# Banded attention before a bilinear feed-forward: from steps of two head pairs by 256 queries to steps of all heads by 128 queries, and from TensorE transposes of the probabilities to 32x32 block transposes on VectorE

## The chip, the cores and the metric

The kernel runs on one core of one Trainium2 chip. The metric is the device time of one execution in microseconds (us). TensorE (PE) multiplies matrices and loads their stationary operand (PEld), VectorE (DVE) and ScalarE (ACT) work element by element on 128 partitions, GpSimd (POOL) is nearly idle here, and SyncE (SP) issues the DMAs of this kernel from one queue, in the order of the program.

## The reference

Attention with a window and a few global keys, whose output, laid out as 3072 tokens by 512 features, is the input of a bilinear feed-forward:

```python
B, H, S, D = 4, 8, 768, 64            # q, k, v: [B, H, S, D], float32
n_global, n_local = 8, 96
scores = (q @ k.T) / sqrt(D)          # per batch and head
rel = pos[:, None] - pos[None, :]
keep = (pos[None, :] < n_global) | ((rel >= 0) & (rel < n_local))
dist = where(is_global & ~is_local, n_local, abs(rel))
scores = where(keep, scores - slopes[h] * dist, -1e9)
a = exp(scores - max(scores)); a = a / (sum(a) + 1e-9)
x = (a @ v).transpose(0, 2, 1, 3).reshape(3072, 512)
out = ((x @ w1) * (x @ w2)) @ w3 @ w_out   # w1, w2: 512x1024, w3: 1024x1024, w_out: 1024x512
```

The weights are float64 on the host and reach the kernel as pairs of 32-bit words.

## The kernel before

**Feed-forward.** `w3 @ w_out` is folded on the chip into one 1024x512 matrix `w` (64 "folds" of 128x512, plain float32, two PE instructions each). Each weight arrives in pieces of 128x512 and is turned into float32 by three DVE passes over it (`convert`, L54, L56 and L58). Every product of activations and weights is made three times, from a high and a low part of both factors (L161 to L163 for `x @ w1` and `x @ w2`, tile `m`; L178 to L180 for the product with the folded matrix, tile `o`). ACT copies `w1h`, `w2h`, `wh` are the high parts of weights, DVE subtractions `w1l`, `w2l`, `wl` (L130, L147) the low ones. `split` makes the high part `xh` of the activations on ACT (L63) and the low part `xl` on DVE (L64). A chunk `c` is 256 tokens. From chunk 2 on the feed-forward takes two chunks (512 tokens) at a time; its program is a generator that is advanced in slices, each of 12 matmuls of 512 columns, so that it fills PE between the parts of the attention. The slices of a block of tokens can begin only when that block's `xh` and `xl` are complete.

**Attention.** It runs in 24 steps `s`, each of 256 queries (one chunk) and two of the four head pairs. A step makes scores on PE (L405: tiles of 64 rows by 64 columns of the PE array, 16 matmuls and 32 PE instructions, since a float32 matmul is two), adds the bias and takes the row extreme on DVE (L420), exponentiates on ACT (L421), inverts the row sums on DVE (L426, L427) and scales the rows on ACT (L433) and DVE (L435). `flip` turns the probabilities by PE transposes against an identity (L445 for the own keys, L447 for the window before them) into PSUM, and ACT copies them out (`ph`, L449). In the next visit PE multiplies them with the values (L468), ACT and DVE add the two halves (`vs`, L503 and L504), and `split` follows.

**What sets the order.** Everything on PE is in the order of the program. In `first_steps` (steps 0 to 3) DVE and SP are as well: there the attention of the first four steps is interleaved with the loads and the conversions of all weights. `ff.weights` gives a list of pieces (`("o", k)`: w_out, `("t", f, half)`: w3, `("w", k)`: w1 and w2), each of which is loaded by SP and then converted by DVE. From step 4 on ACT is in the order of the program, too. Keys and queries (`qr`) and values (`vr`) of a step are loaded by SP; `qr` has two buffers of one head pair each, `vr` four.

## The time and the profile before

| | |
|---|---|
| time of an execution, median of 3 runs | 593.4 us (591.63 to 717.01) |
| span of the profiled execution | 589.8 us, 12652 instructions |
| time of the profiled execution beside its span | no separate time is recorded; the median of the runs is 3.6 us above the span |
| PE busy | 565.4 us, 96% |
| DVE busy | 274.2 us, 46% |
| ACT busy | 297.3 us, 50% |

The span runs from the first instruction to the last. Busy shares are averages over the whole span; the first 98 us, where the weights are converted, are different from the rest, so each stretch has to be looked at by itself.

### The profile page before, as it was taken

To read this page: it belongs to the slowest core of one execution; us is meant where nothing else is said; L and a number is where in the kernel's file an instruction comes from. 1 tells how busy PE (TensorE), PEld (TensorE's weight loads), DVE (VectorE), ACT (ScalarE), POOL (GpSimd) and SP (SyncE) were. 2 spreads that over 40 slices of the span, in tenths; PEclk is the share of its full clock that TensorE was granted. 3 is DMA by queue.
4 is the path that set the end of the run, shared out by engine and by line. 5 is a ranking of instruction groups with operands and counts; after the bars stand their busy time and mean duration, and the time that the engine had idled before them with its cause. 6 is when DMAs were issued, how large, how long until landed. Compare 5 with 4: busy or idle time off the path is not lost.

```text
span 589.8 us, 12652 instructions
## 1 busy us (share of the span) xinstructions
PE 565.4 (96%) x5216; PEld 452.0 (77%) x5216; DVE 274.2 (46%) x875; ACT 297.3 (50%) x801; POOL 1.3 (0%) x10
## 2 busy tenths in 40 slices
PE   2998996999999999999999999999999999999995
PEld 0444556989988888888888888888888888888884
DVE  8999999524444445404534432552244354022200
ACT  3065688446666456536646545663555565322210
POOL 0000000000000000000000000000000000000000
PEclk9999997999999999999999999999999999999999
DMA  8896754202223202212210330221232020100001
GB/s 300 306 359 239 224 217 148 82 21 82 65 80 116 67 15 81 64 55 82 81 57 24 102 114 18 66 64 35 82 116 79 2 82 1 54 19 1 0 36 41
DMA packets 23252, 54.19 MB, mean 92 GB/s; under 512 B 2705, under 2 KB 4753, under 8 KB 23185
## 3 DMA queue, kind: packets, MB, share of 16 engines
q1 hardware_dynamic: 23184, 53.29, 26.6%
q8 instruction: 43, 0.70, 0.5%
q14 instruction: 25, 0.20, 0.1%
HBM read 46.99 MB, written 6.29 MB: 90 GB/s over the span
## 4 chain that ended last, share of the span: by engine, by line
PE 82%; DVE 13%; ACT 2%; DMA 2%; issue 1%; DVEq 0%; ACTq 0%
PE m L161 15%; PE m L162 15%; PE m L163 15%; PE o L178 8%; PE o L179 7%; PE o L180 7%; PE v L468 5%; PE s L405 4%; PE t L445 3%; PE t L447 3%; DVE pr L420 2%; DVE t L58 1%; DVE t L56 1%; DVE t3s L56 1%; DMA stage<-w3t 1%; DVE t3s L58 1%
## 5 line engine op out<-in xcount | busy, mean ns | idle before, releaser
L421 ACT ACTIVATE pr<-pr,mx 128x232 f32<-128x232 f32 (+1 forms) x192 | 88.3, 461 | 23.4 <-DVE mx L420 21.6
L171 DVE TENSOR_TENSOR g<-m,a 128x512 f32<-128x512 f32 x48 | 33.0, 687 | 132.0 <-PE m L163 128.6
L161 PE MATMUL m<-xh,w2h 128*128 128x512 f32 (+1 forms) x224 | 84.4, 377 | 0.0
L161 PE MATMUL m<-xh,w1h 128*128 128x512 f32 (+1 forms) x224 | 81.6, 364 | 0.0
L162 PE MATMUL m<-xl,w1h 128*128 128x512 f32 (+1 forms) x224 | 81.0, 362 | 0.0
L163 PE MATMUL m<-xh,w1l 128*128 128x512 f32 (+1 forms) x224 | 81.0, 361 | 0.0
L162 PE MATMUL m<-xl,w2h 128*128 128x512 f32 (+1 forms) x224 | 80.8, 361 | 0.0
L163 PE MATMUL m<-xh,w2l 128*128 128x512 f32 (+1 forms) x224 | 80.7, 360 | 0.0
L178 PE MATMUL o<-wh,gh 128*128 128x512 f32 x192 | 77.0, 401 | 0.0
L179 PE MATMUL o<-wl,gh 128*128 128x512 f32 x192 | 75.1, 391 | 0.0
L180 PE MATMUL o<-wh,gl 128*128 128x512 f32 x192 | 74.9, 390 | 0.0
L142 PE MATMUL w<-wo,t 128*128 128x512 f32 x128 | 60.6, 623 | 13.1 <-DVE wo L58 11.1
L449 ACT ACTIVATE ph<-t 128x512 f32<-128x512 f32 (+1 forms) x96 | 49.8, 557 | 44.2 <-PE t L447 29.5
L504 DVE TENSOR_TENSOR vs<-v,vs 128x512 f32<-128x512 f32 x24 | 16.6, 690 | 117.2 <-ACT vs L503 117.2
L63 ACT ACTIVATE gh<-g 128x512 fp32r<-128x512 f32 x48 | 30.3, 630 | 68.1 <-DVE g L171 68.1
L142 PEld LDWEIGHTS w<-wo,t 128*128 128x128 f32 x128 | 24.3, 198 | 42.5 <-issue 24.2
L420 DVE CUSTOM_DVE_ANT_0 pr<-s,biasw 128x232 f32<-128x232 f32 x160 | 54.9, 394 | 0.0
L168 ACT ACTIVATE a<-m 128x512 f32<-128x512 f32 x48 | 28.4, 591 | 45.0 <-PE m L163 45.0
L161 PEld LDWEIGHTS m<-xh,w2h 128*128 128x128 f32 x224 | 42.3, 189 | 8.7 <-issue 2.6
L161 PEld LDWEIGHTS m<-xh,w1h 128*128 128x128 f32 x224 | 43.0, 192 | 6.6 <-DVE t3s L58 0.2
L445 PE MATMUL t<-ident,pr 128*128 128x128 f32 x192 | 43.0, 278 | 5.3 <-ACT pr L433 5.2
L162 PEld LDWEIGHTS m<-xl,w1h 128*128 128x128 f32 x224 | 43.0, 192 | 6.4
(84 smaller groups left out, 800.5 us busy)
## 6 DMA issues: line engine op xcount, KB each, us to landing
qr<-qk SPq DMA_DIRECT2D x32, 312.0 KB, 4.4
vr<-vx SPq DMA_DIRECT2D x32, 256.0 KB, 3.5
stage<-w3t SPq DMA_DIRECT2D x15, 512.0 KB, 6.8
out_dram<-ot SPq DMA_DIRECT2D x24, 256.0 KB, 2.0
raws<-w SPq DMA_DIRECT2D x10, 512.0 KB, 6.1
qr<-qk SPq DMA_DIRECT2D x16, 260.0 KB, 4.1
vr<-vx SPq DMA_DIRECT2D x16, 192.0 KB, 3.7
stage<-w SPq DMA_DIRECT2D x6, 512.0 KB, 7.1
```

What stands on the lines that cost most here:

```text
L142: nc.tensor.matmul(ps, lhsT=self.t3[f, z][:, i * P:(i + 1) * P].bitcast(F32), rhs=self.wo[:, k].bitcast(F32), start=k == 0, stop=k == NFC - 1)
L161: nc.tensor.matmul(ps[:, z], lhsT=mh, rhs=xh[:, i], start=i == 0, stop=False)
L162: nc.tensor.matmul(ps[:, z], lhsT=mh, rhs=xl[:, i], start=False, stop=False)
L163: nc.tensor.matmul(ps[:, z], lhsT=ml, rhs=xh[:, i], start=False, stop=i == NCC - 1)
L171: nc.vector.tensor_tensor(out=g, in0=ps, in1=a, op=ALU.mult)
L178: nc.tensor.matmul(ps, lhsT=gh[:, f, ts], rhs=self.wh[:, f], start=f == 0, stop=False)
L179: nc.tensor.matmul(ps, lhsT=gh[:, f, ts], rhs=self.wl[:, f], start=False, stop=False)
L180: nc.tensor.matmul(ps, lhsT=gl[:, f, ts], rhs=self.wh[:, f], start=False, stop=f == NFC - 1)
L420: nc.vector.tensor_tensor_reduce(out=pr[:, j, u, w0:], in0=ps[u][:, j, w0:UW], in1=bias, scale=-SCALE, scalar=3.0e38, op0=ALU.add, op1=ALU ...
L421: nc.scalar.activation(pr[:, j, u, w0:], pr[:, j, u, w0:], AF.Exp, bias=m, scale=-1.0, accum_out=sm[:, j, u:u + 1])
L445: nc.tensor.transpose(pt[:, u, 0], pr[:, j, u, BW:UW], ident)
L449: nc.scalar.activation(ph[:, :, :nk], pt[:, :, :nk], AF.Copy)
```

## The change

A step now is 128 queries of all eight heads. The 128 rows of a score tile are 4 head pairs by 32 queries; a "quarter" `q` is one of the four groups of 32 queries, each with its own frame of 136 keys (8 global and 128 of the window). There are still 24 steps. A step makes 32 score matmuls (64 PE instructions) with 64 rows and 32 columns of the array each and 136 streamed columns (32, 64, 96 and 128 in the first step of a batch), and 8 passes of 128x136 on DVE (L435) and ACT (L436). The probabilities are scaled by one DVE pass over 128x8x136 (in steps 0 to 3 by eight ACT copies, L455) and turned by two DVE instructions in 32x32 blocks (L461, STREAM_TRANSPOSE, 128x4x5x32 each). The values are multiplied in seven windows of 32 keys and the globals, with 32 rows and 64 columns of the array: 64 matmuls, 128 PE instructions of 32 to 128 columns (32 matmuls in the first step of a batch). They accumulate in the same four PSUM banks (`sc`) that held the scores, and `split` reads them from there. The PE transposes, the copies `ph`, and the copy and the addition `vs` are gone.

`qr`, `vr`, `pt` and `pr` have one buffer each. The load of keys and queries is one DMA of up to 1.38 MB, the one of values of .52 MB; `load_keys(s + 1)` is issued right behind `scores(s)` and waits for them. `tokens(s - 1)`, the split of a step's values, stands behind the rows of the next step.

```diff
@@ -28,15 +28,17 @@
 NFC = DF // P
 WIN = 96
 GLB = 8
-SLOT = GLB + P
-KW = WIN + NQ * SLOT
-BW = WIN + GLB
-UW = BW + P
-QW = KW + T
-STEP = 2
+R = 32
+NR = P // R
+KF = P + GLB
+KW = NR * KF
+QW = KW + P
+PW = P + R
+NB = S // P
+OWN = (NR - 1) * KF
+NV = 2 * NR - 1
 PC = 512
 HF = NFC // 2
-HQ = P // 2
 W = 2 * T
 SLOPES = [2.0 ** -(h + 1) for h in range(H)]
 FAR = 2.0 ** 38
@@ -74,7 +76,7 @@
         self.w3t, self.w_out, self.out = w3t, w_out, out
         self.wp = wp = ctx.enter_context(tc.tile_pool(name="wp", bufs=1))
         self.mp = ctx.enter_context(tc.tile_pool(name="mp", bufs=2))
-        self.ps = ctx.enter_context(tc.tile_pool(name="ps_m", bufs=2, space=PSUM))
+        self.ps = ctx.enter_context(tc.tile_pool(name="ps_m", bufs=4, space=PSUM))
         self.w = [[wp.tile([P, NFC, NCC, P], F32R, name=f"w{n}{x}") for x in "hl"] for n in (1, 2)]
         self.wh, self.wl = (wp.tile([P, NFC, DO], F32R, name=n) for n in ("wh", "wl"))
 
...
+def strided(ap, *dims):
+
+    return bass.AP(ap.tensor, ap.offset, [ap.ap[0], *dims])
+
+
 @with_exitstack
 def banded(ctx, tc, ff, ns, nt, nf, oki, ident, qk, vx):
 
...
+    at = ctx.enter_context(tc.tile_pool(name="at", bufs=1))
+    ps = ctx.enter_context(tc.tile_pool(name="ps_a", bufs=1, space=PSUM))
+
+    sc = ps.tile([P, 4, 512], F32, name="sc")
+    pr = bp.tile([P, NR, 2, PW], F32, name="pr")
+
...
+    def load_keys(s):
+        b, t = divmod(s, NB)
+        k0 = 0 if t else OWN
+        q = at.tile([P, NP, QW], F32, tag="qr", name=f"qr_{s}")
+        nc.sync.dma_start(out=q[:, :, k0:], in_=qk[b, t, :, :, k0:])
+        return q
+    def load_values(s):
+        b, t = divmod(s, NB)
+        i0, i1 = (0, NV + 1) if t else (NR - 1, NV)
+        v = at.tile([P, NV + 1, P], F32, tag="vr", name=f"vr_{s}")
+        nc.sync.dma_start(out=v[:, i0:i1], in_=vx[b, t, :, i0:i1])
+        return v
+    def frame(s, q):
+        return (0, KF) if s % NB else (WIN - R * q, P)
+    def scored(u, q, w0, w1):
+        k = P + q % 2 * KF
+        return slice(None), 2 * u + q // 2, slice(k + w0, k + w1)
+    def scores(s):
+        m = qrs[s]
+        for q in range(NR):
+            w0, w1 = frame(s, q)
+            k0 = q * KF if s % NB else OWN - w0
+            for hp in range(NP):
                 for u in range(2):
+                    rows = slice(u * D, (u + 1) * D)
+                    _, i, cols = scored(u, q, w0, w1)
+                    nc.tensor.matmul(sc[hp * R:(hp + 1) * R, i, cols], lhsT=m[rows, hp, KW + q * R:KW + (q + 1) * R], rhs=m[rows, hp, k0 + w0:k0 + w1], start=True, stop=True)
+    def rows(s, q):
+        w0, w1 = frame(s, q)
+        mx, sm = stats[s]
+        for u in range(2):
+            bias = biasw[:, u, w0:w1] if s % NB else bias0[:, u, q, w0:w1]
+            x, m = pr[:, q, u, w0:w1], mx[:, q, u:u + 1]
+            nc.vector.tensor_tensor_reduce(out=x, in0=sc[scored(u, q, w0, w1)], in1=bias, scale=-SCALE, scalar=3.0e38, op0=ALU.add, op1=ALU.min, accum_out=m)
+            nc.scalar.activation(x, x, AF.Exp, bias=m, scale=-1.0, accum_out=sm[:, q, u:u + 1])
+    def all_rows(s, between=None):
+        stats[s] = [at.tile([P, NR, 2], F32, tag=t, bufs=2, name=f"{t}_{s}") for t in ("mx", "sm")]
+        for q in range(NR):
+            rows(s, q)
+            if between:
+                between()
+    def probabilities(s, scaled):
+        sm = stats[s][1]
         nc.vector.tensor_scalar(out=sm, in0=sm, scalar1=1e-9, scalar2=None, op0=ALU.add)
         nc.vector.reciprocal(out=sm, in_=sm)
+        if scaled is nc.scalar:
+            for q in range(NR):
+                w0, w1 = frame(s, q)
+                for u in range(2):
+                    x = pr[:, q, u, w0:w1]
+                    nc.scalar.activation(x, x, AF.Copy, scale=sm[:, q, u:u + 1])
+        else:
+            x = pr[:, :, :, :KF]
+            nc.vector.tensor_tensor(out=x, in0=x, in1=strided(sm, [2, NR], [1, 2], [0, KF]), op=ALU.mult)
+        pts[s] = pt = at.tile([P, 2, NV + 1, P], F32, tag="pt", name=f"pt_{s}")
         for u in range(2):
+            nc.vector.transpose(strided(pt[:, u], [P + R, NR], [P, NR + 1], [1, R]), pr[:, :, u].rearrange("p q (k c) -> p q k c", c=R))
+    def values(s):
+        pt, v = pts.pop(s), vrs.pop(s)
+        parts = []
+        if s % NB:
+            parts.append((NV, 0, NR, lambda x, u: strided(x[:, u, NR], [P + R, NR], [1, R])))
+        for i in range(NR - 1 if s % NB == 0 else 0, NV):
+            q0, q1 = max(0, i - NR + 1), min(NR, i + 1)
+            parts.append((i, q0, q1, lambda x, u, i=i, q0=q0, q1=q1: x[:, u, i, q0 * R:q1 * R]))
+        for n, (i, q0, q1, of) in enumerate(parts):
+            for hp in range(NP):
+                rows = slice(hp * R, (hp + 1) * R)
                 for u in range(2):
+                    cols = slice(u * D, (u + 1) * D)
+                    nc.tensor.matmul(sc[cols, hp, q0 * R:q1 * R], lhsT=v[rows, i, cols], rhs=of(pt[rows], u), start=n == 0, stop=n == len(parts) - 1, skip_group_check=True)
+    n = B * NB
     work = []
+    qrs, vrs, pts, stats, xs = {}, {}, {}, {}, {}
     def slices(k):
         while k > 0 and work:
...
             else:
                 k -= 1
     def visit(s):
         if s:
+            values(s - 1)
+        if s < n:
+            scores(s)
+            if s + 1 < n:
+                qrs[s + 1] = load_keys(s + 1)
+            vrs[s] = load_values(s)
+    def tokens(s):
+        if s % 4 == 0:
+            xs[s // 4] = [xp.tile([P, NCC, W], F32R, tag=tag, name=f"{tag}_{s // 4}") for tag in ("xh", "xl")]
+        x2 = xs[s // 4]
+        i = s % 4 * P
+        split(nc, *(x[:, :, i:i + P] for x in x2), sc[:, :, :P])
+        c = s // 2
+        if s % 2 and c < 2:
+            work.append(ff.run(c, *(x[:, :, c * T:(c + 1) * T] for x in x2), c * T, T))
+        elif s % 4 == 3:
+            work.append(ff.run(c, *x2, (c - 1) * T, W))
...
         ff.weights(("t", 1, 1), ("t", 2, 1))
-        loads(0, vals=False)
+        qrs[0] = load_keys(0)
         ff.weights(("o", 4), ("o", 5))
-        ps = visit(0)
+        visit(0)
         for k in (4, 5):
             for f in range(3):
                 ff.fold(f, k)
         ff.weights(("o", 6), ("o", 7))
-        loads(0, keys=False)
-        prs = all_rows(0, ps)
+        all_rows(0)
...
-        def scale(s):
-            for p, r in zip(pairs(s), prs):
-                softmax(*p, *r, nc.scalar)
-            loads(s + 1)
-        def fold_and_turn(f, s):
-            ff.fold(f, 0, 1, 2, 3)
-            turn(s, 0, prs)
-            ff.fold(f, 4, 5, 6)
-            turn(s, 1, prs)
-            ff.fold(f, 7)
+        def step(s):
+            visit(s)
+            all_rows(s)
+            tokens(s - 1)
         w3(3)
-        scale(0)
+        probabilities(0, nc.scalar)
         ff.low(0)
         w3(4)
         ff.low(1)
         ff.low(2)
         w3(5)
         w12(0)
-        fold_and_turn(3, 0)
+        ff.fold(3, *range(NFC))
         ff.lows()
         w3(6)
-        prs = all_rows(1, visit(1))
+        step(1)
         ff.low(3)
         ff.fold(4, *range(NFC))
         w12(1)
-        scale(1)
+        probabilities(1, nc.scalar)
         ff.lows()
         w3(7)
         ff.low(4)
-        fold_and_turn(5, 1)
+        ff.fold(5, *range(NFC))
         w12(2)
         ff.lows()
         ff.low(5)
-        prs = all_rows(2, visit(2))
+        step(2)
         ff.fold(6, *range(NFC))
         w12(3)
-        scale(2)
+        probabilities(2, nc.scalar)
         ff.lows()
         ff.low(6)
-        fold_and_turn(7, 2)
+        ff.fold(7, *range(NFC))
         w12(4)
         ff.lows()
         w12(5)
         ff.lows()
         ff.low(7)
-        prs = all_rows(3, visit(3))
+        step(3)
         w12(6)
         slices(2)
-        scale(3)
+        probabilities(3, nc.scalar)
         ff.lows()
         w12(7)
-        slices(SLICES[3][0] - 2)
-        ff.lows()
-        for i in range(STEP):
-            turn(3, i, prs)
-            slices(SLICES[3][i + 1])
+        slices(2)
+        ff.lows()
+        slices(6)
         fits(nc, ff.mp, nf, oki)
-    SLICES = [()] * 3 + [(4, 4, 2)] * 3 + [(4, 2, 2)] * 2 + [(5, 4, 3)] * (n - 8)
+    SLICES = [0] * 3 + [10] * 3 + [8] * 2 + [12] * (n - 8)
     with tc.manual_schedule(engines={mybir.EngineType.PE}):
         with tc.manual_schedule(engines={mybir.EngineType.DVE, mybir.EngineType.SP}):
             first_steps()
         with tc.manual_schedule(engines={mybir.EngineType.Activation}):
-            for s in range(4, n + 1):
-                rs = all_rows(s, visit(s))
-                if s == n:
-                    break
+            for s in range(4, n):
+                visit(s)
+                all_rows(s, lambda: slices(1))
+                tokens(s - 1)
                 slices(2)
-                for p, r in zip(pairs(s), rs):
-                    softmax(*p, *r, nc.vector)
-                loads(s + 1)
-                slices(SLICES[s][0] - 2)
-                for i in range(STEP):
-                    turn(s, i, rs)
-                    slices(SLICES[s][i + 1])
+                probabilities(s, nc.vector)
+                slices(SLICES[s] - NR - 2)
+            visit(n)
+            tokens(n - 1)
             slices(10 ** 6)
...
```

Three places show how rows moved. The first is SP's queue in the first stage, where the keys and queries of step 1 (in the kernel after: `qr_257`) and the last two pieces of w_out (`stage_xh<-w_out`) are loaded. In the kernel before:

```order
L50 DMA stage<-w_out 128x1024 [waits DMAHW5_49,DVE_49]
L50 DMA stage<-w_out 128x1024 [waits DMAHW6_49,DVE_49]
L50 DMA stage_xh<-w_out 128x1024 [waits DMAHW7_49,DVE_49]
L50 DMA stage_xh<-w_out 128x1024 [waits DMAHW0_49,DVE_49]
L390 DMA vr_0_262<-vx 128x384 [waits DMAHW1_49]
L390 DMA vr_1_264<-vx 128x384 [waits DMAHW2_49]
L50 DMA stage<-w3t 128x1024 [waits DMAHW5_49,DMAHW3_49,DVE_49]
L50 DMA stage<-w3t 128x1024 [waits DMAHW6_49,DMAHW4_49,DVE_49]
L383 DMA qr_2_319<-qk 128x520 [waits PE_49]
```

and in the kernel after:

```order
L397 DMA qr_215<-qk 128x4x264 [waits DMAHW3_49]
L52 DMA stage<-w_out 128x1024 [waits DMAHW4_49,DVE_49]
L52 DMA stage<-w_out 128x1024 [waits DMAHW5_49,DVE_49]
L397 DMA qr_257<-qk 128x2688 [waits DMAHW6_49,DMAHW3_49,PE_49]
L404 DMA vr_259<-vx 128x512 [waits DMAHW7_49]
L52 DMA stage_xh<-w_out 128x1024 [waits DMAHW0_49,DVE_49]
L52 DMA stage_xh<-w_out 128x1024 [waits DMAHW1_49,DVE_49]
L52 DMA stage<-w3t 128x1024 [waits DMAHW4_49,DMAHW2_49,DVE_49]
```

The load of the next keys now stands ahead of the two w_out pieces and waits for PE; before, the next keys (`qr_2_319`) came behind them.

The second place is DVE around the inversion of step 1's row sums (`sm`), between two weight conversions. Before:

```order
L56 SCALAR_TENSOR_TENSOR t3s<-raws,t3s 128x512 [waits DVE_49] x2
L58 SCALAR_TENSOR_TENSOR t3s<-raws,t3s 128x512 [waits DVE_49] x2
L426 TENSOR_SCALAR sm_2_465<-sm_2_465 128x4 [waits Activation_49]
L427 RECIPROCAL sm_2_465<-sm_2_465 128x4 [waits DVE_49]
L426 TENSOR_SCALAR sm_3_476<-sm_3_476 128x4 [waits Activation_49]
L427 RECIPROCAL sm_3_476<-sm_3_476 128x4 [waits DVE_49]
L130 TENSOR_TENSOR w1l<-t3s,w1h 128x512 [waits Activation_49]
L130 TENSOR_TENSOR w2l<-t3s,w2h 128x512 [waits Activation_49]
```

and after:

```order
L58 SCALAR_TENSOR_TENSOR t3s<-raws,t3s 128x512 [waits DVE_49] x2
L60 SCALAR_TENSOR_TENSOR t3s<-raws,t3s 128x512 [waits DVE_49] x2
L448 TENSOR_SCALAR sm_449<-sm_449 128x8
L449 RECIPROCAL sm_449<-sm_449 128x8 [waits DVE_49]
L461 STREAM_TRANSPOSE pt_501<-pr 128x4x5x32 [waits Activation_49] x2
L132 TENSOR_TENSOR w1l<-t3s,w1h 128x512
L132 TENSOR_TENSOR w2l<-t3s,w2h 128x512
```

Two block transposes of the probabilities, which wait for ACT's scaling, now stand between the reciprocal and the low parts of the weights.

The third place is ACT at step 12, the first visit after the last values of a block of 512 tokens. Before (`vs_2` and `xh` are the values of step 11, `pr` the rows of step 12, `ot_3` the last output of the feed-forward block that is being finished, `a_0` the first copy of the next):

```order
L503 ACTIVATE vs_2_3023<-v_5_2_2958 128x512
L63 ACTIVATE xh_2258<-vs_2_3023 128x2x256
L421 ACTIVATE pr_0_3028,sm_0_3030<-pr_0_3028,mx_0_3029 128x128 x2
L421 ACTIVATE pr_0_3028,sm_0_3030<-pr_0_3028,mx_0_3029 128x232 x2
L421 ACTIVATE pr_1_3039,sm_1_3041<-pr_1_3039,mx_1_3040 128x128 x2
L421 ACTIVATE pr_1_3039,sm_1_3041<-pr_1_3039,mx_1_3040 128x232 x2
L184 ACTIVATE ot_3_3062<-o_3_2944 128x512
L433 ACTIVATE pr_0_3028<-pr_0_3028,sm_0_3030 128x128
L433 ACTIVATE pr_0_3028<-pr_0_3028,sm_0_3030 128x232
L433 ACTIVATE pr_1_3039<-pr_1_3039,sm_1_3041 128x128
L433 ACTIVATE pr_1_3039<-pr_1_3039,sm_1_3041 128x232
L168 ACTIVATE a_0_3100<-m_0_0_3087 128x512
```

and after:

```order
L436 ACTIVATE pr,sm_2887<-pr,mx_2886 128x32 x2
L436 ACTIVATE pr,sm_2887<-pr,mx_2886 128x64 x2
L436 ACTIVATE pr,sm_2887<-pr,mx_2886 128x96 x2
L436 ACTIVATE pr,sm_2887<-pr,mx_2886 128x128 x2
L185 ACTIVATE ot_3_2929<-o_3_2892 128x512
L65 ACTIVATE xh_2280<-sc 128x4x128
L169 ACTIVATE a_0_2949<-m_0_0_2936 128x512
```

The high part `xh` of the last values moved from ahead of the exponentials to behind them and behind `ot_3`.

## Rows read from the trace of the kernel before

**Rows 1.** The page: busy time, share of the span and instructions of each engine, and the busy tenths of PE and DVE in 40 slices of 14.7 us.

```profile
PE 565.4 (96%) x5216; PEld 452.0 (77%) x5216; DVE 274.2 (46%) x875; ACT 297.3 (50%) x801; POOL 1.3 (0%) x10
...
PE   2998996999999999999999999999999999999995
...
DVE  8999999524444445404534432552244354022200
```

**Rows 2.** The page: the chain of work that ended last, shares of the span by engine.

```profile
PE 82%; DVE 13%; ACT 2%; DMA 2%; issue 1%; DVEq 0%; ACTq 0%
```

**Rows 3.** Windows of the whole span; the columns are the stretch, its length, busy us (and instructions) of PE, PEld, DVE, ACT and POOL, the granted clock, the DMA share and GB/s.

```profile
0.00:98.00 98.00, 80.06 (x568) 42.16 (x568) 92.54 (x240) 51.10 (x147) 1.33 (x10) 0.99 0.76 270
...
111.00:515.00 404.00, 403.96 (x4238) 340.71 (x4240) 160.46 (x596) 224.38 (x615) 0.00 (x0) 1.00 0.20 65
```

**Rows 4.** The timeline of PE at the second transposes of a step; start and length in us, line, operation, tiles, count. Lengths overlap, so the pitch is read from the starts.

```profile
299.47 0.39 PE L163 MATMUL m<-xh,w2l 128*128 128x512 f32 x1
299.70 0.49 PE L445 MATMUL t<-ident,pr 128*128 128x128 f32 x3
...
300.25 0.27 PE L447 MATMUL t<-ident,pr 128*128 128x128 f32 x1
300.27 0.48 PE L161 MATMUL m<-xh,w2h 128*128 128x512 f32 x1
300.59 0.40 PE L162 MATMUL m<-xl,w2h 128*128 128x512 f32 x1
```

**Rows 5.** Groups by line and form: the PE transposes; count, then busy us, mean ns, and idle us before them with its releaser.

```profile
L445 PE MATMUL t<-ident,pr 128*128 128x128 f32 x192 | 43.0, 278 | 5.3 <-ACT pr L433 5.2
L447 PE MATMUL t<-ident,pr 128*128 128x128 f32 x160 | 38.5, 276 | 0.0
```

**Rows 6.** The timeline of SP's queue: the issue of the last two w_out pieces.

```profile
16.64 0.93 SPq L50 DMA_DIRECT2D stage_xh<-w_out  x2
```

**Rows 7.** The timeline of PE in the first stage: the scores of step 0, the folds behind them, and the first transpose of step 3; in brackets the idle time before an instruction and its releaser.

```profile
25.38 1.24 PE L405 MATMUL s<-qr 64*64 64x64 f32 x32
...
26.55 14.00 PE L142 MATMUL w<-wo,t 128*128 128x512 f32 x32
...
98.42 0.47 PE L445 MATMUL t<-ident,pr 128*128 128x128 f32 x1 [4.67 <-ACT pr L433]
```

**Rows 8.** Windows of PE alone: stretch, length, busy us (instructions), granted clock, DMA share, GB/s.

```profile
13.60:25.40 11.80, 11.80 (x25) 1.00 0.94 367
98.42:103.20 4.78, 4.78 (x23) 0.50 0.02 3
```

**Rows 9.** The chain in order of time: start, length, what.

```profile
0.75 3.03 DMA nt<-ns
...
113.91 0.32 PE m L161
...
409.48 1.30 PE v L468 x63
410.78 1.01 PE s L405 x25
...
450.69 1.56 PE v L468 x96
452.25 1.14 PE s L405 x32
```

**Rows 10.** The timeline of DVE in the first stage: conversion of the last two w_out pieces, the first rows of step 0, the end of step 0's softmax and two waits for weights behind it, and the ends of the softmax of steps 1 and 3.

```profile
26.38 0.75 DVE L54 TENSOR_SCALAR wo<-stage_xh 128x512 int32<-128x512 int32 x2
...
28.26 1.29 DVE L58 SCALAR_TENSOR_TENSOR wo<-stage_xh,wo 128x512 int32<-128x512 int32 x2
29.46 0.28 DVE L420 CUSTOM_DVE_ANT_0 pr<-s,bias 128x128 f32<-128x128 f32 x1
...
35.22 0.66 DVE L147 TENSOR_TENSOR wl<-w,wh 128x512 fp32r<-128x512 f32 x1
...
36.67 0.43 DVE L54 TENSOR_SCALAR t<-stage 128x512 int32<-128x512 int32 x1 [0.46 <-DMA stage<-w3t]
...
41.32 0.43 DVE L54 TENSOR_SCALAR t<-stage 128x512 int32<-128x512 int32 x1 [0.28 <-DMA stage<-w3t]
...
60.00 0.66 DVE L130 TENSOR_TENSOR w1l<-t3s,w1h 128x512 fp32r<-128x512 f32 x1
...
97.70 0.18 DVE L427 RECIPROCAL sm<-sm 128x4 f32<-128x4 f32 x1
```

**Rows 11.** The timeline of ACT in the first stage: one exponential, the eight scalings of step 2, one high part of a weight.

```profile
30.57 0.47 ACT L421 ACTIVATE pr<-pr,mx 128x232 f32<-128x232 f32 x1
...
78.69 3.13 ACT L433 ACTIVATE pr<-pr,sm 128x232 f32<-128x232 f32 x8
...
97.36 0.63 ACT L122 ACTIVATE w2h<-t3s 128x512 fp32r<-128x512 f32 x1
```

**Rows 12.** Groups by line and form: the output copy on ACT and the split of the values on ACT and DVE.

```profile
L184 ACT ACTIVATE ot<-o 128x512 f32<-128x512 f32 x24 | 14.2, 590 | 29.9 <-PE o L180 27.6 <-ACT ph L449 2.3
L63 ACT ACTIVATE xh<-vs 128x512 fp32r<-128x512 f32 x24 | 15.2, 632 | 22.8 <-DVE vs L504 22.8
L64 DVE TENSOR_TENSOR xl<-vs,xh 128x512 fp32r<-128x512 f32 x24 | 16.6, 692 | 3.7 <-ACT xh L63 2.8
```

More of the change, by code (lines that the diff above doesn't have):

```diff
@@ new lines, in biases @@
+        n = KF + NR * GLB
+        it = bp.tile([P, n], I32, name="it")
+        gi = bp.tile([P, NR * GLB], I32, name="gi")
+        qi = bp.tile([P, 1], I32, name="qi")
+        qf = bp.tile([P, 1], F32, name="qf")
+        sl = bp.tile([P, 2], F32, name="sl")
+        rel, loc, dist = (bp.tile([P, n], F32, name=x) for x in ("rel", "loc", "dist"))
+        keep, more = (bp.tile([P, NR * GLB], F32, name=x) for x in ("keep", "more"))
+        win, glob, own = slice(0, P), slice(P, KF), slice(KF, n)
@@ new lines, in biases @@
+        for h in range(H):
+            hp, u = divmod(h, 2)
+            nc.gpsimd.memset(sl[hp * R:(hp + 1) * R, u:u + 1], -SLOPES[h] / SCALE)
+        nc.gpsimd.memset(pr, 0.0)
+        nc.vector.tensor_scalar(out=qi, in0=qi, scalar1=R - 1, scalar2=None, op0=ALU.bitwise_and)
+        nc.vector.tensor_copy(out=qf, in_=qi)
+        nc.vector.tensor_copy(out=nf, in_=nt)
+        nc.vector.tensor_scalar(out=rel, in0=it, scalar1=qf, scalar2=None, op0=ALU.add)
+        nc.vector.tensor_scalar(out=keep, in0=gi, scalar1=ng, scalar2=None, op0=ALU.is_lt)
@@ L393, in scores @@
-    def scores(c, hp, qr):
-        ps = sc[hp % STEP]
-        for j in range(NQ):
-            w0 = BW if c % NCB == 0 and j == 0 else 0
-            for g in range(P // HQ):
-                cols = slice(max(w0, g * HQ), BW + (g + 1) * HQ)
-                q0 = KW + j * P + g * HQ
-                for u in range(2):
-                    m = qr[u * D:(u + 1) * D]
-                    nc.tensor.matmul(ps[u][g * HQ:(g + 1) * HQ, j, cols], lhsT=m[:, q0:q0 + HQ], rhs=m[:, j * SLOT:][:, cols], start=True, stop=True)
-        return ps
@@ L424, in softmax @@
-    def softmax(c, hp, pr, sm, scaled):
+        nc.vector.tensor_scalar(out=dist[:, glob], in0=keep[:, :GLB], scalar1=nl, scalar2=None, op0=ALU.mult)
+        nc.vector.tensor_tensor(out=keep, in0=keep, in1=loc[:, own], op=ALU.max)
+        nc.vector.tensor_tensor(out=more, in0=keep, in1=loc[:, own], op=ALU.subtract)
+        nc.vector.scalar_tensor_tensor(out=dist[:, own], in0=more, scalar=nl, in1=dist[:, own], op0=ALU.mult, op1=ALU.add)
+        nc.vector.tensor_copy(out=loc[:, own], in_=keep)
@@ L436, in softmax @@
-        return pr
-    def flip(c, hp, j, pr):
-        first = c % NCB == 0 and j == 0
-        nk = 1 if first else 2
-        pt = ps_v.tile([P, 2, 2, P], F32, tag="v", name=f"t_{c}_{hp}_{j}")
-        for u in range(2):
-            nc.tensor.transpose(pt[:, u, 0], pr[:, j, u, BW:UW], ident)
-            if not first:
-                nc.tensor.transpose(pt[:, u, 1], pr[:, j, u, 0:P], ident)
-        ph = at.tile([P, 2, 2, P], F32, tag="ph", bufs=4, name=f"ph_{c}_{hp}_{j}")
-        nc.scalar.activation(ph[:, :, :nk], pt[:, :, :nk], AF.Copy)
-        return ph
@@ L452, in values @@
-    def values(uu, c, hp, vr, phs):
-        lo, hi, both = slice(0, HQ), slice(HQ, P), slice(0, P)
-        for j, ph in enumerate(phs):
-            own, win = (j, 0), (2 * NQ - 1 - j, 1)
-            if c % NCB == 0 and j == 0:
-                seqs = [[(own, r, both, True, True)] for r in (lo, hi)]
-            else:
-                back = slice(HQ, BW)
-                seqs = [[(own, lo, hi, True, True), (own, lo, lo, True, False), (win, lo, lo, False, True)],
-                        [(win, back, lo, True, True), (own, hi, hi, True, False), (win, back, hi, False, True)]]
-            for parts in zip(*seqs):
-                for u in range(2):
-                    rows = slice(u * D, (u + 1) * D)
-                    for r, ((i, k), keys, q, start, stop) in enumerate(parts):
-                        nc.tensor.matmul(uu[r][rows, j * P:][:, q], lhsT=vr[keys, i, rows], rhs=ph[keys, u, k, q], start=start, stop=stop)
```

158 lines of the change are left out of this document (31 added, 127 removed).

## The prediction, made before the changed kernel ran

> **What bounds the kernel now.** I read the page first: PE is busy 96% of the span and its tenths are full from the eighth slice on, while DVE's are full only in the first seven [rows 1]. The chain of waits says the same by shares: PE 82%, DVE 13% [rows 2]. Cut into stretches, there are two regimes [rows 3]: from 111 to 515 us PE is busy 403.96 of 404.00 us, so there each us taken from PE or put on it counts in full; in the first 98 us DVE is busy 92.54, converting weights, and what is put on DVE there, or makes it wait, counts, and what PE does is mostly covered. A behaviour of the middle stretch that no share shows: DVE (160 us) and ACT (224) idle there, which is free only as long as PE has other work queued.
>
> **The change part by part.** The sum is made against the profiled span of 589.8 us; the median of the runs is 593.4, 3.6 above it, and I add that at the end.
>
> *1. The PE transposes.* Between two `m` matmuls, six transposes lengthen the stretch from 299.47 to 300.59 to 1.12 us [rows 4]. Two matmuls at their pitch of .23 (299.47 to 299.70) account for .455, so six cost .665, or .11 each, refill included. There are 192 + 160 = 352 of them [rows 5]; 56 belong to steps 0 to 3 and lie in the DVE stretch. 296 x .11 = **-32.6 us**, all on the path.
>
> *2. The first stage.* Here the order of SP and DVE decides. Before, the last two w_out pieces are issued at 16.64 [rows 6], long ahead of their conversion at 26.38. After, the load of step 1's keys stands ahead of them, and with one buffer it waits for the scores of step 0, which start at 25.38 and end by about 26.4 [rows 7]. Then 1.38 MB of keys, .26 of values and two pieces of .52 are queued: 2.69 MB at the 367 GB/s of a full queue [rows 8] take 7.3 us, and a short load takes 3.0 to land [rows 9]: 36.7. The conversion of the two pieces, 3.1 us from 26.38 to 29.46 [rows 10], overlaps the second landing a little and ends at 39.4: **+10.0** for everything behind it on DVE.
>
> PE's folds wait with it. The earlier ones are 12 instructions at 14.0/32 = .44 us from 26.55, so PE is dry from 31.8 to 38.8, when the first piece is ready. Before, a PE that had waited 4.67 us [rows 7] came back at a granted clock of .50 (1.2 of 2.4 GHz) for 4.8 us [rows 8]. The 12 instructions of the next folds then take 4.8 us for the first 5.4 of them and 2.9 for the rest and end at 46.4; ACT copies the last fold (.6) and makes the last scaling (.4), for which the two block transposes wait on DVE. No row has a block transpose. Its nearest relatives are conversion passes of 512 elements: .34 at best (L54's two in .75, less their overlap) and .60 (the pitch from 28.26 to 29.46) [rows 10]; for 640 elements .42 and .75, and twice that if it takes two passes. I take .75, by the pass nearest to it in reading and writing all of its data. DVE goes on at 48.9 instead of 35.22, +13.7; two waits for weights of before (.46 and .28 [rows 10]) are swallowed: +13.0.
>
> In each of steps 1 to 3 DVE before went straight from the reciprocal to `w1l` at 60.00 [rows 10]. Now it waits until ACT has made two high parts (.60 pitch of a .63 instruction) and eight scalings (.30 each, the shorter rows taken from eight in 3.13 [rows 11]), 2.85 us beyond what it does meanwhile, and then turns 2 x .75; one small pair of instructions less saves .2: +4.2 per step. The `xl` behind the rows waits for ACT's exponentials: +.65 in step 1, +.2 in steps 2 and 3. The two weight pieces behind the keys of step 3 (1.9 MB, issued after scores that are themselves late): +1.3 in step 2. Sum on DVE: 13.0 + 4.85 + 5.7 + 4.4 = 27.9, so the transposes of step 3 end at 97.70 + 27.9 = 125.6. Behind them stand two low parts (1.2) and a conversion (3.1), then the `g` (.7) that frees a PSUM buffer for the `m` matmul that in both programs follows the scores of step 4. It comes at 130.8 instead of 113.91 [rows 9]: **+16.9**, I take +17. PE's own work of before between 98 and 111 is done in the meantime. Bounds: +11 with the cheapest transposes and no cold PE; +23 with two passes and slower loads.
>
> *3. Where a block of tokens begins.* `xh` of step s-1 now stands on ACT behind the rows of step s and behind `ot_3`, which waits for the last slice of the old block. At steps 12, 16 and 20 PE has four slices (5.5 us) behind the scores, then nothing it may start until ot (.59), xh (.63) and xl (.69) [rows 12] are made: with hand-overs 2.0 us each, where PE never waited before [rows 3]. At step 8 only two slices are left behind the scores, 2.7 us, while eight exponentials (.38 pitch of a .47 instruction [rows 11]), ot, xh and xl need some 7.0: 4.3, and up to 2.4 more of low clock, as PE had after its pause of 4.67 us [rows 7, 8]. Sum 10.3 to 12.7, **+11**; 0 if DVE and ACT run ahead of my order, 13 at worst. The last block needs no such wait, since its rows are over.
>
> *4. Scores and values on PE.* Before, a step costs 1.56 + 1.14 us, or 1.30 + 1.01 where a batch begins [rows 9]: 14 x 2.70 + 6 x 2.31 = 51.7 in steps 4 to 23. After, there are 17 x 192 + 3 x 128 = 3,648 instructions, each with its weights, and I allow .53 a step for filling and switching. The fastest row of small ones is 96 in 1.56, .28 of it fill: 13.3 ns each, with four tiles of the array at work. At that rate 48.5 + 10.6 = 59.1: +7. If instead columns decide (32 scores of 140 columns in 1.14, 35 ns each on four tiles, is .83 ns a column in each tile; 64 columns on four tiles give just 13.3), then eight tiles take 8.3 ns for a value and 14.2 for a score, and the sum is 47: -4. Since no row is faster than 13.3 ns, I lean to the upper end: **+3**.
>
> Rows show 16 ns for a pair of load and matmul, fill included [rows 9]. The Trainium skill, page "TensorE: Matmul & The Clock Gate", section "Wait — 56ns, not 53.3ns?", says that starts are never closer than about 25 ns however few columns. By that rule term 4 would be about +50 us instead of +3; this trace contradicts it for tiles of 64x64, and no row shows tiles of 32 rows.
>
> *5. Hidden.* DVE after the first stage does less per step than before (about 8.5 of 19.5 us), ACT loses `ph`, `vs` and most scalings; both had slack [rows 3], and PE's queue covers them. The loads of 1.9 MB per step need 5.2 us at 367 GB/s of some 19: hidden by PE's slices, at a cost of up to 5 us per step if not.
>
> **Sum:** -32.6 + 17 + 11 + 3 = -1.6; 588.2 for the span, **592 us** beside the runs of before.
>
> **The rivals.** *A, the added waits stay hidden.* The -32.6 holds, but SP's wait costs a few us only, since another queue order or earlier landing covers it, and block beginnings are covered by slices still queued: what is left of +28 is 5 to 8. For it: PE's backlog is full at all block boundaries before [rows 3]. Against it: the order of SP, DVE and ACT in the new program is fixed at just these places. Time 593.4 - 23 = 570.
>
> *B, slower: small pairs run at an issue rate.* Place: the 192 load and matmul pairs of each step, where tiles have 32 rows or 32 columns; every step's pairs are on PE's path. Price: 3.65 us per ns over 13.3. The slowest row of small pairs is 35 ns (32 scores in 1.14 us [rows 9]); halfway to it, at 24 ns, term 4 is +46 and the time 635. It decides from about 16 ns on, where the whole is 2% slower. For it: half again as many instructions per step, most with fewer columns. Against it: the 13.3 of the row of values. By the rule cited above, 25 ns, the time would be 639.
>
> *C, the eight tiles do not run at once*, because tiles that share rows of the array take turns: two scores at once are 57 ns each, 3.6 us a step, four values at once 17 ns each, 2.1, some 60 us in all, 650. Against it: the four tiles of before share two groups of rows and ran at a quarter.
>
> *D, the transposes take two passes*, 1.5 us each: +1.5 per step in the first stage, +6 in all, 598; the change then still is within 2%. That the change does not do what it says can be left out: the transposes are gone from the order of PE.
>
> **How the numbers follow.** My forecast with D: .48. A: .25. B: .20. C: .05; the rest, .02, is split. Two per cent (12 us) is about what a measurement of this kernel can tell from no change. Within it lie 581.5 to 605.3. The forecast's own range, from the bounds of terms 2 to 4 (-6 to +6, -4 to +2, -7 to +4), combined as independent, is 583 to 602. For 8 in 10 I take 569 on the side of A, which leaves out less than half of it, and 618 on the side of B, which leaves out rates above 19 ns. Faster by over 2%: .25; within: .48; slower: .27, as the upper bounds of terms 2 and 4 together also pass 605.
>
> **What would show it.** In the trace after: no PE transposes, and PE's busy time in the steady steps lower by about 30; the two w_out pieces landing at about 37 instead of before 26, and PE idle some 7 us before the folds that need them, then .50 of the clock; the wait of the block transposes for ACT's scalings, and their duration near .75; the first `m` behind the scores of step 4 at about 131; PE idle for 2 us, three times, and some 4 once, before the first `m` of a block, released by `xl`; scores and values together 2.6 to 2.9 us a step. The forecast is wrong if the first stage ends within a few us of 114, if the pairs need 16 ns or more, or if the loads of 1.4 MB keep PE waiting at each score.

## The result and the profile after

The changed kernel is a little slower: 595.9 us (median of 4) against 592.8, a ratio of 1.0067 with a 95% interval of 1.0043 to 1.0090. The forecast was 592, no change. One of the four executions of the kernel before was slow (717.0 us) and is left out of the ratio. The profiled span of the changed kernel is 592.9 us against 589.8.

From the page after, beside [rows 1] and [rows 2]:

```profile
PE 538.7 (91%) x6400; PEld 423.2 (71%) x6400; DVE 273.6 (46%) x788; ACT 187.0 (32%) x591; POOL 2.9 (0%) x20
...
PE   2959597979999799999999998999979999999995
...
DVE  7759687885354343533355413535233454112200
...
PE 74%; DVE 13%; ACT 5%; DMA 4%; issue 2%; SPq 1%; ACTq 0%; DVEq 0%
```

PE lost 26.7 us of work (565.4 to 538.7), and the span grew all the same: PE now has holes. What fills them is in the waits of PE, whose columns are the waiting line, what it waited for, us in total, times and the longest. PE over the whole span:

```profile
PE w L143 <- DVE wo L60: 17.4, 2, 10.6
PE sc L478 <- DVE pt L461: 14.7, 5, 7.1
PE sc L426 <- issue: 6.6, 6, 1.6
PE m L162 <- ACT xh L65: 6.4, 4, 2.7
PE m L163 <- DVE xl L66: 2.1, 4, 1.4
```

The first two lines are the first stage (10.6 of them is the start of the program, as before), the last two the beginnings of blocks of tokens, and the third is one that the forecast does not have: PE stands in the middle of a step's scores, and nothing that this list names holds it. Five of its six waits are over 1 us, at steps 14, 15, 20, 21 and 22; they are called stalls below.

The end of the first stage, beside 113.91 in [rows 9]: the first `m` behind the scores of step 4, on PE's timeline.

```profile
126.77 0.39 PE L162 MATMUL m<-xh,w2h 128*128 128x256 f32 x1
```

It comes 12.9 us later, and the end of PE's work 3.0 us later (586.8 against 583.8). So the rest of the program runs 9.9 us faster than before, where the transposes alone should have given over 30.

The waits of DVE from 30 to 130 us say what lengthened the first stage:

```profile
DVE pt L461 <- ACT pr L455: 9.8, 4, 2.5
DVE wo L56 <- DMA stage_xh<-w_out: 9.1, 2, 8.2
DVE xl L66 <- ACT xh L65: 6.8, 3, 2.3
DVE t3s L56 <- DMA stage<-w: 1.3, 2, 0.9
DVE gl L66 <- ACT gh L65: 0.7, 1, 0.7
```

And the steady steps, from the chain of waits in order of time, beside 450.69 and 452.25 in [rows 9]: values and scores of one undisturbed step, then of step 14 with a stall.

```profile
249.14 1.74 PE sc L478 x87
250.88 1.13 PE sc L426 x64
...
308.45 1.74 PE sc L478 x87
310.19 0.62 PE sc L426 x32
310.82 1.34 issue
312.16 0.70 PE sc L426 x32
```

A full step costs 1.74 + 1.13 = 2.87 us where it cost 2.70. (The x87 counts only what the chain went through; the values of a full step have 128 instructions, and the trace has them all.)

### The profile page after: what moved, and what is told of

Its sections match the earlier page's. It is cut to its first block, busy times and chain, and to the rows that moved or that the text cites. A ratio compares the mean times of both kernels' runs of the same rounds, so it can differ in the third digit from the quotient of the medians.

```text
span 592.9 us, 14620 instructions
## 1 busy us (share of the span) xinstructions
PE 538.7 (91%) x6400; PEld 423.2 (71%) x6400; DVE 273.6 (46%) x788; ACT 187.0 (32%) x591; POOL 2.9 (0%) x20
## 4 chain that ended last, share of the span: by engine, by line
PE 74%; DVE 13%; ACT 5%; DMA 4%; issue 2%; SPq 1%; ACTq 0%; DVEq 0%
PE m L163 14%; PE m L162 14%; PE m L164 14%; PE o L179 7%; PE o L181 7%; PE o L180 7%; PE sc L478 6%; PE sc L426 4%; ACT pr L436 2%; PE w L143 2%; DVE pt L461 1%; ACT pr L455 1%; DVE t3s L58 1%; DMA stage<-w 1%; DMA stage_xh<-w_out 1%
## 5 line engine op out<-in xcount | busy, mean ns | idle before, releaser
L436 ACT ACTIVATE pr<-pr,mx 128x136 f32<-128x136 f32 (+2 forms) x192 | 74.2, 388 | 83.0 <-DVE mx L435 83.0
L162 PE MATMUL m<-xh,w2h 128*128 128x512 f32 (+1 forms) x224 | 80.7, 360 | 0.0
L143 PEld LDWEIGHTS w<-wo,t 128*128 128x128 f32 x128 | 25.5, 205 | 51.0 <-issue 28.0
L435 DVE CUSTOM_DVE_ANT_0 pr<-sc,biasw 128x136 f32<-128x136 f32 x160 | 37.0, 295 | 50.5 <-PE sc L426 50.5
L478 PEld LDWEIGHTS sc<-pt,vr 32*64 32x64 f32 x2816 | 40.8, 140 | 24.8 <-DVE pt L461 17.5
L478 PE MATMUL sc<-pt,vr 32*64 32x32 f32 (+3 forms) x2816 | 44.5, 260 | 14.7 <-DVE pt L461 14.7
L164 PEld LDWEIGHTS m<-xh,w1l 128*128 128x128 f32 x224 | 42.7, 191 | 6.4
L163 PEld LDWEIGHTS m<-xl,w2h 128*128 128x128 f32 x224 | 42.3, 189 | 6.3
```

What stands on the lines that cost most here:

```text
L143: nc.tensor.matmul(ps, lhsT=self.t3[f, z][:, i * P:(i + 1) * P].bitcast(F32), rhs=self.wo[:, k].bitcast(F32), start=k == 0, stop=k == NFC - 1)
L162: nc.tensor.matmul(ps[:, z], lhsT=mh, rhs=xh[:, i], start=i == 0, stop=False)
L163: nc.tensor.matmul(ps[:, z], lhsT=mh, rhs=xl[:, i], start=False, stop=False)
L164: nc.tensor.matmul(ps[:, z], lhsT=ml, rhs=xh[:, i], start=False, stop=i == NCC - 1)
L435: nc.vector.tensor_tensor_reduce(out=x, in0=sc[scored(u, q, w0, w1)], in1=bias, scale=-SCALE, scalar=3.0e38, op0=ALU.add, op1=ALU.min, acc ...
L436: nc.scalar.activation(x, x, AF.Exp, bias=m, scale=-1.0, accum_out=sm[:, q, u:u + 1])
```

## The experiments

The theory after these readings: the transposes bring what was forecast; the order of SP's queue and the waits of DVE for ACT cost about 13 us in the first stage, the place of `tokens` about 12 at the beginnings of blocks, and the stalls in the scores 6 to 8. Rivals are named with each run. Times are medians in us; ratios are to the kernel before, run beside each, and differences from the kernel after are taken from the ratios (its own is 1.0067).

**The w_out pieces first (e1).**

```diff
-        visit(0)
+        scores(0)
...
         ff.weights(("o", 6), ("o", 7))
+        qrs[1] = load_keys(1)
+        vrs[0] = load_values(0)
         all_rows(0)
```

> The kernel after, with the loads of the last two w_out pieces issued ahead of the keys and values that follow the scores of step 0; all else as it is. Theory (the late pieces start the delay of the first stage): PE's pause of 6.9 us before the folds that need them goes, with the low clock behind it, and the first m matmul behind the scores of step 4, at 126.8 in the kernel after, comes 8 to 11 us earlier; time 585 to 589. Rival (the block transposes and their waits for ACT's scalings make the delay, or the loads behind are late in turn): the pause goes, but that m matmul comes less than 4 us earlier; time 592 to 596.

Measured: 589.7, ratio 0.9975 (0.9961 to 0.9989), so about 5.5 us less than the kernel after. PE's pause of 6.9 us before the folds falls to 1.7, as expected. The first `m` behind the scores of step 4 comes at 120.93 instead of 126.77, 5.8 earlier: between the two expectations. DVE's waits from 30 to 130 us show why:

```profile
DVE pt L461 <- ACT pr L455: 9.4, 4, 2.5
DVE xl L66 <- ACT xh L65: 6.8, 3, 2.3
DVE t L56 <- DMA stage<-w3t: 4.6, 2, 3.7
```

The 9.1 us for w_out became 4.6 for the next pieces, of w3, which stand behind the keys. So about half of this wait came from the order; the other half moved to the next pieces, behind the load of a step's keys in one piece. That a smaller load would take it away was not tried.

**The scaling of steps 0 to 3 on DVE (e5).**

```diff
-        probabilities(0, nc.scalar)
+        probabilities(0, nc.vector)
...
-        probabilities(3, nc.scalar)
+        probabilities(3, nc.vector)
```

> The kernel after, with the probabilities of steps 0 to 3 scaled by one DVE pass each, as from step 4 on, instead of by eight ACT copies. Theory (DVE's four waits of 2.4 to 2.5 us before the block transposes, for ACT's scalings, lengthen the first stage one for one): the waits go, 1.3 us of DVE per step comes in their place, the first m behind the scores of step 4 comes 4 to 5 us earlier; time 590 to 592. Rival (the loads set the end of the first stage, so that DVE then waits for weights instead): that m moves by less than 2 us; time 594 to 597.

Measured: 591.4, ratio 0.9991 (0.9974 to 1.0007), 4.5 us less than the kernel after; the first `m` behind the scores of step 4 comes at 120.50, 6.3 us earlier. The wait of `pt` for ACT is gone from DVE's list, and no wait for weights has taken its place:

```profile
DVE wo L56 <- DMA stage_xh<-w_out: 8.5, 2, 7.6
DVE xl L66 <- ACT xh L65: 6.9, 3, 2.3
```

So in this stage a wait of DVE is paid about one for one: four times 2.45, less four passes of 1.29, is 4.6. A trace tells it to about 1 us only: in the kernel after, e2 and e4, whose first stage has the same program, that `m` stands at 126.77, 125.69 and 125.65.

**The split ahead of the next rows (e2).**

```diff
                 visit(s)
-                all_rows(s, lambda: slices(1))
                 tokens(s - 1)
+                all_rows(s, lambda: slices(1))
```

> The kernel after, with the split of a step's values (xh, xl) ahead of the rows of the next step from step 4 on. Theory (PE runs dry where a block of tokens begins because xh stands on ACT behind the exponentials and the last output copy): the pauses before the first m of a block at 193, 277, 359 and 440 us (4.1, 1.4, 1.5, 1.4 us by the trace) and the low clock behind the first go; 8 to 12 us less, time 584 to 588. Rival (ACT and DVE are too full there, and the rows now come late in their place): the pauses move to the values that wait for the block transposes; time 593 to 598.

Measured: 576.4, ratio 0.9743 (0.9726 to 0.9759), 19 us less than the kernel after: more than expected, in the direction of the theory. The waits of PE from 130 to 530 us, first in the kernel after e2:

```profile
PE sc L426 <- issue: 2.6, 2, 1.6
PE o L179 <- ACT gh L65: 0.3, 1, 0.3
```

All waits for `xh` and `xl` are gone and none came in their place. Three of five stalls are gone as well, which nobody had asked for. Counted as gaps this makes 8.5 + 4.0 us; a gap understates its price, as PE's timeline at step 12 of the kernel after shows:

```profile
276.49 0.39 PE L181 MATMUL o<-wh,gl 128*128 128x512 f32 x1
278.10 0.50 PE L162 MATMUL m<-xh,w1h 128*128 128x512 f32 x1 [1.22 <-ACT xh L65]
278.83 0.50 PE L163 MATMUL m<-xl,w1h 128*128 128x512 f32 x1 [0.22 <-DVE xl L66]
```

At the pitch of .23 the third line would start at 276.95: 1.9 us are lost, where the two gaps say 1.44, since a matmul's length is about double its pitch. At step 8 it is the same with larger numbers, and the clock falls:

```profile
192.81 0.39 PE L181 MATMUL o<-wh,gl 128*128 128x512 f32 x1
195.92 0.50 PE L162 MATMUL m<-xh,w1h 128*128 128x512 f32 x1 [2.73 <-ACT xh L65]
197.81 0.80 PE L163 MATMUL m<-xl,w1h 128*128 128x512 f32 x1 [1.39 <-DVE xl L66]
...
197.80:201.20 3.40, 3.39 (x8) 0.51 0.00 0
```

(the last line is a window: 3.4 us at a granted clock of .51). That is 4.5 us to the third line and 1.6 for the clock. With 1.9 at each of steps 12, 16 and 20 the four beginnings cost 11.8 us. Taken in the same way, by the scores of the five steps (2.67, 2.80, 3.15, 2.59 and 2.56 us instead of 1.13), the stalls cost 8.1 us in the kernel after, and 3.2 in e2 (2.35 and 3.11 us at steps 20 and 21). Together 16.7. The profiled spans differ by 18.3 (592.9 and 574.6), of which 1.1 lies in the first stage, whose program e2 leaves as it is; about .5 us is open.

**A slice between values and scores (e3).**

```diff
         if s:
             values(s - 1)
+        if between:
+            between()
         if s < n:
             scores(s)
...
-                visit(s)
+                visit(s, lambda: slices(1))
...
-                slices(SLICES[s] - NR - 2)
+                slices(SLICES[s] - NR - 3)
```

> The kernel after, with one slice of 12 feed-forward matmuls between the values of a step and the scores of the next, from step 4 on, and one less behind the probabilities. Theory (PE works off its small instructions, 192 pairs in 2.9 us, faster than its instructions arrive): the five stalls in the middle of scores (1.1 to 1.6 us, waits for nothing that the profile shows) go or fall under .3 us in all; 5 to 7 us less, time 589 to 591. Rival (the load of the values, issued in the same moment, holds the instruction fetch up): the stalls stay, though elsewhere; time 594 to 597.

Measured: 592.3, ratio 1.0013 (0.9999 to 1.0028), 3.2 us less than the kernel after. No stall is left:

```profile
PE m L162 <- ACT xh L65: 7.2, 4, 3.5
PE m L163 <- DVE xl L66: 2.1, 4, 1.4
PE sc L478 <- DVE pt L461: 0.5, 1, 0.5
```

The slice, as the timeline shows it at step 10, is six matmuls of 512 columns and 1.6 us; "12" in the section on the kernel before and in the expectation holds only for the matmuls of 256 columns of the first two chunks.

```profile
230.91 1.80 PE L478 MATMUL sc<-pt,vr 32*64 32x128 f32 x128
232.64 0.50 PE L162 MATMUL m<-xh,w2h 128*128 128x512 f32 x1
...
233.93 0.39 PE L164 MATMUL m<-xh,w2l 128*128 128x512 f32 x1
234.24 1.20 PE L426 MATMUL sc<-qr 64*32 64x136 f32 x64
```

The stalls go as the theory says, the time falls less than it says: an undisturbed step now is 19.65 us from scores to scores (234.24 to 253.89) against 19.42 (231.40 to 250.81), some 5 us over 20 steps. That this is the price of going from small to large tiles and back once more is likely, but no run separates it.

**The load of the values later (e4).**

```diff
-        with tc.manual_schedule(engines={mybir.EngineType.Activation}):
+        with tc.manual_schedule(engines={mybir.EngineType.Activation, mybir.EngineType.SP}):
```

> The kernel after, with SP in the order of the program from step 4 on, so that the load of the values stands behind that of the next keys, which waits for the scores: no load is issued while the small matmuls run. Theory of the instruction rate: the stalls in the middle of scores stay, 5 to 7 us in all; time 594 to 597. Rival (the load holds the instruction fetch up): the stalls go; time 588 to 591.

Measured: 595.7, ratio 1.0065 (1.0046 to 1.0085), as the kernel after. The waits of PE from 130 to 530 us:

```profile
PE sc L426 <- issue: 6.6, 6, 1.6
PE m L162 <- ACT xh L65: 6.4, 4, 2.7
```

The stalls stay, at the same steps and with the same number of scores left (32, 40, 18, 26 and 35 of 64). That the load of the values holds PE up is out.

**64 pairs more, once (e9).** The places of the stalls drift: between steps 14 and 15, and from 20 over 21 to 22, each comes some 8 pairs earlier in the scores. A full step has 192 pairs of load and matmul in values and scores and 72 in its slices, 264 = 2 x 128 + 8. Counted through the whole program, the numbers of the pairs at the five stalls leave 88, 88, 86, 86 and 85 when divided by 128. So the stalls sit on every 128th pair, where it falls into the scores with a full step of values ahead. This was put to a test:

```diff
             scores(s)
+            if s == 4:
+                scores(s)
```

> The kernel after, with the scores of step 4 made twice (the second writes the same numbers over the first): 64 more pairs of load and matmul once, 1.1 us, and nothing else moved. Theory (the stalls come where every 128th pair falls on pairs 20 to 50 of a step's scores, with a full step of values ahead; the places of the stalls in the kernel after and in e2 and e3 fit this count): the stalls at steps 14, 15, 20, 21 and 22 go, and at most two come, at steps 6 and 12; time 591 to 594. Rival (the stalls belong to these steps for another reason, such as the loads or outputs that run there): five stalls as before; time 596 to 598.

Measured: 598.9, ratio 1.0109 (1.0082 to 1.0135), 2.5 us more than the kernel after. The five stalls are gone from steps 14, 15, 20, 21 and 22, and stand at steps 6, 10, 11, 12 and 18 (PE's timeline, the instructions behind each; the last count is the scores that are left, and at step 10 the scores are just over):

```profile
163.10 0.60 PE L426 MATMUL sc<-qr 64*32 64x96 f32 x28 [1.00 <-issue]
...
236.41 0.50 PE L164 MATMUL m<-xh,w1l 128*128 128x512 f32 x1 [0.83 <-issue]
...
256.97 0.43 PE L426 MATMUL sc<-qr 64*32 64x136 f32 x7 [1.59 <-issue]
...
278.42 0.45 PE L426 MATMUL sc<-qr 64*32 64x128 f32 x15 [2.07 <-issue]
...
403.28 0.29 PE L426 MATMUL sc<-qr 64*32 64x128 f32 x1 [1.65 <-issue]
```

Their numbers leave 92, 90, 89, 89 and 87. The count moved them all, so they belong to the stream of instructions and not to what runs beside it. The forecast of the time was wrong: I had taken pairs 20 to 50 for the window in which a 128th pair hurts, and it reaches to the end of the scores, so steps 10, 11 and 18 (pairs 57 and later) had one, too; of the 2.5 us, 1.1 are the second scores. In the profiled execution, whose span is 4.4 us longer than that of the kernel after, the granted clock was also at .50 for some 3.4 us more at each of three places (from 201, 280 and 368 us). The count also explains what e2 did to the stalls: at step 8 its next block is there in time for two slices that the kernel after has nothing to fill with, so all later scores stand 12 pairs later in the count, and the 128th pairs of steps 14, 15 and 22 fall on pairs 20, 12 and 20 of the scores, too early for a stall (the scores of step 14 still take 1.49 us instead of 1.13).

**The removal alone (e6).**

```diff
-            nc.tensor.transpose(pt[:, u, 0], pr[:, j, u, BW:UW], ident)
-            if not first:
-                nc.tensor.transpose(pt[:, u, 1], pr[:, j, u, 0:P], ident)
...
-        nc.scalar.activation(ph[:, :, :nk], pt[:, :, :nk], AF.Copy)
+        x = pr[:, j, :, BW if first else 0:UW]
+        x = bass.AP(x.tensor, x.offset, [x.ap[0], [UW, 2], [BW, nk], [1, P]])
+        nc.scalar.activation(ph[:, :, :nk], x, AF.Copy)
```

> The kernel before, without the PE transposes: ACT copies the probabilities straight from SBUF into the tile that held the turned ones, so the values are multiplied with probabilities that are not turned (this part of the computation is left out). It is the removal alone, without what the change puts in its place. Theory (each of the 296 transposes of steps 4 to 23 costs PE .11 to .12 us on the path, those of steps 0 to 3 are covered by DVE): 32 to 36 us less, time 556 to 561. Rival (the gain was smaller from the start, since PE's neighbours cover part of it): 20 to 28 us less, time 564 to 572.

Measured: 557.1, ratio 0.9412 (0.9389 to 0.9435): 34.8 us less than before. The gain was there in full. In the profiled spans it is 35.3 us (589.8 to 554.5), of which 1.8 lies ahead of the first `m` behind the scores of step 4 (112.03 against 113.84 on the timeline) and 33.5 behind it.

**Together (e7, e8).** e7 has the edits of e1, e2, e3 and e5, and the split ahead of the rows in steps 1 to 3 as well; e8 is e7 without the slice of e3.

> The kernel after with the four edits together: the last w_out pieces loaded ahead of the keys, one slice between values and scores, the split of the values ahead of the next rows in all steps, and the probabilities of steps 0 to 3 scaled on DVE. Theory (these are separate costs on the path, nearly additive): 561 to 567. Rival (what one edit frees another wait takes, above all in the first stage, where loads may set the end): 570 to 576.

Measured: 566.1, ratio 0.9571 (0.9552 to 0.9591).

> e7_all_four without the slice between values and scores. The slice took the stalls away in e3, but its steps are longer (19.65 us against 19.42 between two scores), so it may cost as much as it brings. Theory (two stalls come back, at steps 20 and 21 as in e2, 2.6 us, and 20 times .25 us for going from small to large tiles and back once more go): 562 to 565. Rival (the stalls come back at five or more steps): 568 to 571.

Measured: 564.9, ratio 0.9533 (0.9516 to 0.9551). The two stalls are back at steps 20 and 21, PE's only waits from 130 to 530 us:

```profile
PE sc L426 <- issue: 2.9, 2, 1.6
```

e8 beats both kernels, the one before by 4.7% and the one after by 5.3%. The costs add up nearly: from 595.9, less 5.5, 4.5 and 19, would be 567; whether the split of the early steps makes the rest was not tried by itself. The trace of e8 agrees part by part: the first `m` behind the scores of step 4 comes at 113.88, as before (113.84), so the first stage costs nothing any more, and from there to the end of the span e8 takes 26.7 us less than the kernel before, where the transposes (-33.5), scores and values (+2.6, see below) and two stalls (+3.5) make -27.4.

## Why the prediction was wrong

The sum was -1.6 us, measured +3.1 (span). Term by term:

- *The PE transposes:* -32.6 forecast, -33.5 behind the first stage by e6. Right.
- *The first stage:* +17 forecast, +12.9 measured; the mechanisms are the ones named, the sizes off in both directions. The w_out pieces are issued at 27.42 and DVE waits 9.1 us for them (forecast 10.0 later); PE pauses 6.86 (7.0) and the clock falls for less than the 4.8 us of the forecast (.69 granted from 37.7 to 42.5, so some 3 us at the lower level); the transposes wait 2.45 us (2.85) and take .8 each (.75). The wait of `xl` is the one sized worst: 2.3 instead of .7 in each of three steps, where .65, .2 and .2 were added. Undoing two of these waits gave 5.5 and 4.5 back (e1, e5).
- *Beginnings of blocks:* +11 forecast, 11.8 by the timeline, and e2 took all these waits away. Right.
- *Scores and values:* +3 forecast; 17 x 2.87 + 3 x 1.83 (.95 and .88 where a batch begins) = 54.3 against 51.7 is +2.6. The 128 instructions of the values in 1.74 us are 13.6 ns each, right at the fastest row of before, and the 64 of the scores in 1.13 us 17.7. The rule of 25 ns (the Trainium skill, "TensorE: Matmul & The Clock Gate", section "Wait — 56ns, not 53.3ns?"), weighed in the prediction, does not hold for these tiles of 32 rows by 64 columns either: the trace shows about half of it.
- *Hidden:* right. From 130 to 530 us PE waits for nothing of DVE, ACT or the loads but for the beginnings of blocks and once .3 us.
- *Not in the sum:* the stalls of PE, 8.1 us. -33.5 + 12.9 + 11.8 + 2.6 + 8.1 = +1.9, within 1.2 us of the measured +3.1.

The step that failed is term 4: I priced the small instructions, half again as many per step as before, per pair, as a rate, and concluded from the rate of before that they are nearly free. The rate held (2.87 us for 192 pairs, 14.9 ns each, filling included), and PE still stopped once in a while; that was in no term and in no rival, and it cost 8.1 us. The other four terms sum to -6.2 where I had -1.6, which is inside the bounds I gave them; the missing term turned the sign. That 592 came within 4 us of 595.9 is luck: the first stage, put 4.1 us too high, made up for half of the missing term.

Some slips in the working moved nothing that mattered. The 160 and 224 us of DVE and ACT in [rows 3] are their busy times, so they idle 244 and 180. A column at .83 ns is what the row of the values gives (13.3 x 4 / 64); the scores' own row gives 1.0 (35 x 4 / 140). The bounds as stated, combined as independent, give 582 to 599 and not 583 to 602, and that of term 3 goes down to 0 in its own paragraph, not to 7.

Of the rivals, A (the waits stay hidden) fell: each wait stood where the order said. B and C fell with the 13.6 and 17.7 ns. D fell with the .8 us of a block transpose. With another order the waits of the first stage and of the blocks can be hidden: e8 does it, at 565.

## What to carry to other kernels

A removal on the bound engine is worth its full price only if the new order keeps that engine fed: here some 33 us were earned and 35 given back, 25 of them at places that one can read from the order of the instructions beforehand, who stands behind whom on SP, ACT and DVE. Take a consumer's input (here `xh` and `xl`) out of a queue behind work that itself ends late, and look at loads that grow by being merged and at what is queued behind them. Count the bound engine's instructions, too: a burst of very short ones can outrun their delivery even where their mean rate is fine.
